# Q's and K's projections: interleaving pairs of heads in the matmul's output instead of in the cast

## The chip, the cores and the metric

The kernel runs on one core of a Trainium2 chip. The metric is the device time of one execution in microseconds, as a median over runs.

## The reference

Two branches read the same `x` (2048 rows of 512) and are mixed by a gate. Branch A is attention with a recurrent memory: 64 segments of 32 rows, 32 heads of 128, and 8 memory rows that each segment's output hands to the next.

```python
for s in range(n_seg):                       # 64 segments, one after the other
    xs = x[:, s * seg_len:(s + 1) * seg_len, :]
    h = jnp.concatenate([mem, xs], axis=1)   # 8 + 32 rows
    q = jnp.einsum('btd,dhe->bhte', h, Wq)   # 32 heads, 128 wide
    k = jnp.einsum('btd,dhe->bhte', h, Wk)
    v = jnp.einsum('btd,dhe->bhte', h, Wv)
    scores = jnp.einsum('bhqe,bhke->bhqk', q, k) * scale
    scores = jnp.where(mask, scores, -1e9)
    p = softmax(scores)
    o = jnp.einsum('bhqk,bhke->bhqe', p, v)
    o = jnp.einsum('bhte,hed->btd', o, Wo)
    mem = o[:, :M, :]                        # the next segment's memory
    outs.append(o[:, M:, :])
a = concatenate(outs)
b = gelu(layernorm(x) @ w1 + b1) @ w2 + b2
g = sigmoid((x * gate_w).sum(-1))
out = g * a + (1 - g) * b
```

## The kernel before

**Stages.** Branch B (layer norm, two matmuls, gelu) runs first, in blocks of 256 rows, while the attention weights are loaded; its result goes to `c_dr` in DRAM. Towards its end the first rows of the attention are projected between its matmuls. Then comes a loop over the 64 segments (`for s in range(nseg)`), grouped into 16 tiles `T` of four segments `si`. The order of instructions on every engine is the order of the program; no scheduler moves anything.

**Rows of a segment.** A segment has 8 + 32 = 40 rows, and a quarter of TensorE's columns takes 32. So the 8 memory rows and 24 of the segment's rows go through the loop directly (`hT`), and the other 8 rows of each of a tile's four segments, 32 in all, go together as left-over rows (`GL`). These are projected one tile ahead, as filling work between the steps of the segments: `left_qk` in the first and second segment of a tile, the output projection of the left-over rows (`wo_left`) in the third, `left_v` in the fourth.

**The projection of Q and K.** `qk_unit` (L110) computes one half (16 heads) of Q or K for 32 rows, with the rows as the stationary operand and the weights streaming through. The 128 elements of a head are cut into four parts `j` of 32, and each part has a quarter of the array's columns of its own: matmul `j` writes 512 words to partitions 32j to 32j + 31 of one PSUM bank, for 16 heads times 32 elements. Four matmuls `j` make a group, and four groups (`kc`, the four slices of 512 model columns) add up to a unit of sixteen matmuls. A segment has four units: Q and K of the first half of the heads, then Q and K of the second, in banks `U0` to `U3`. The left-over rows take four units per tile, in `X1` and `X2` (for the first tile also `U0`).

**Cast and transpose.** `qk_cast` (L115, ScalarE) casts a unit's bank to a bfloat16 tile `Tb`, in which the elements of two neighbouring heads alternate: layout (pair, element, head of the pair). In PSUM the two heads lie one after the other, 32 words each. The cast reads each partition in order and writes with a step of two elements. `qk_tr` (L119, VectorE) then transposes `Tb` as 32 x 32 blocks of four-byte words, a word being a pair of heads, into `QT` or `KT` (or `QL`; `kl_tr` at L125 into `KL` for left-over rows). Later matmuls read one head of a pair with a step of two.

**The rest of a segment, in the order of TensorE.** Mask and scores of the first half (L248, L256, L260, bank `SbF`); V's first half and a part of its second (L129); scores of the second half (bank `W`); the rest of V; the sums of the exponentials (L267, L270); P times V (L280, L285); the output projection (L141, bank `W`); the mask into `SbF`; filling work; the transposed memory rows for the next segment (L696), which take the cast `w` of the output projection (L609, ScalarE) and give `hT` (L697, VectorE), on which the next segment's L110 waits. In the first segment of a tile `out_sel` (L226), in the fourth `x_mm` (L156) stands ahead of L696. Reciprocals of the sums (L590, L655) run on VectorE; GpSimd multiplies the segment's rows by them (L601, L602), after they have been spread through DRAM (`r_dr`, `Rb`).

Of the kernel before, what the change touches and what calls it, by code (L numbers as in the profile page):

```python
# [27 lines left out]
def kernel(ctx, tc, A_x, A_mem0, A_Wq, A_Wk, A_Wv, A_Wo, A_seg_len, B_x, B_w1, B_b1, B_w2, B_b2, gate_w, out):  # L28
    nc = tc.nc
# [73 lines left out]
    W5 = (Wq5, Wk5)  # L103
# [3 lines left out]
    def qk_unit(bk, G, t, hf, kc):  # L107
        h0, h1 = HF[hf]
        for j in range(4):
            nc.tensor.matmul(bk[32 * j:32 * j + 32, :], lhsT=G[:, kc, :], rhs=W5[t][:, kc, h0:h1, j, :],  # L110
                             start=(kc == 0), stop=(kc == KC - 1), tile_position=(0, 32 * j))

    def qk_cast(bk):
        Tb = ew.tile([P, 8, 32, 2], BF16, tag="Tb", bufs=3, name="Tb")
        nc.scalar.copy(out=Tb[:].rearrange("p a e b -> p a b e"), in_=bk.rearrange("p (a b e) -> p a b e", a=8, b=2))  # L115
        return Tb

    def qk_tr(Tb, dst, hf):
# [52 lines left out]
    def left_qk(T, t, hf, bk):  # L171
        for kc in range(KC):
            qk_unit(bk, gl(T), t, hf, kc)
            if kc < KC - 1:
                yield
        def ca():
            Tb = qk_cast(bk[:])
            dve_q.append(lambda: qk_tr(Tb, QL[T % 2], hf) if t == 0 else kl_tr(Tb, T, hf))
        act_q.append(ca)
        yield  # L180
# [432 lines left out]
    for s in range(nseg):  # L613
# [17 lines left out]
        for n, (t, hf) in enumerate(((0, 0), (1, 0), (0, 1), (1, 1))):  # L631
            bk = U[n]
            for kc in range(KC):
                qk_unit(bk, hc, t, hf, kc)
            if n == 0:
                flush(act_q, 9)
                mask_mm(1)
                flush(dve_q, 9)
            qk_tr(qk_cast(bk[:]), (QT, KT)[t], hf)
# [226 lines left out]
```

## Time and profile before

| | before |
|---|---|
| median of 3 runs | 811.36 us (809.99 to 811.54) |
| the profiled execution | 808.66 us |
| its span, first to last instruction | 806.9 us |
| granted TensorE clock, mean | 0.996 |
| busy: PE / PE weight loads | 770.5 / 417.2 us |
| busy: ACT / DVE / POOL | 579.7 / 441.9 / 253.2 us |

PE is TensorE, PEld its weight loads (which overlap with its matmuls), ACT ScalarE, DVE VectorE, POOL GpSimd. Busy time counts stretches in which an engine has at least one instruction under way, so four matmuls side by side count once. The time of an execution stands beside its span: 1.8 us lie around it.

### The profile page before, as it was taken

The numbers are of one execution on the slowest core, as the hardware profiler recorded it, in microseconds if no ns is written. First come the engines' busy times: TensorE is split into PE (matmuls) and PEld (weight loads), VectorE is DVE, ScalarE is ACT, GpSimd is POOL, SyncE is SP. The second block draws the span as 40 slices with busy tenths as digits, with TensorE's granted clock in tenths as the row PEclk, the third lists the DMA queues.
The fourth block names the chain that finished last, engine by engine and source line by source line (L and its number), as shares of the span: only waits on it lengthen the run. The fifth ranks groups of instructions, "written<-read, shape, count | busy, mean of one in ns | idle before, by whom it ended". The sixth has DMA issues, their size and how long they took to land.

```text
span 806.9 us, 41225 instructions
## 1 busy us (share of the span) xinstructions
PE 770.5 (95%) x18390; PEld 417.2 (52%) x18418; DVE 441.9 (55%) x1059; ACT 579.7 (72%) x1442; POOL 253.2 (31%) x377
## 2 busy tenths in 40 slices
PE   6888999999999999999999999999999999999996
PEld 4555644555555555555555555555555555555543
DVE  5764445564646555655555565546555655555554
ACT  4554677777777777777777777877777777777773
POOL 3000013333333333333333333332333333333331
PEclk9999999999999999999999999999999999999999
DMA  6996011212122121212121222222111212121111
GB/s 190 389 381 204 28 43 48 69 63 75 69 67 77 50 66 60 85 59 85 59 84 50 61 69 76 69 70 75 57 59 59 86 60 84 60 78 59 55 57 56
DMA packets 38950, 70.41 MB, mean 87 GB/s; under 512 B 3947, under 2 KB 29136, under 8 KB 37232
## 3 DMA queue, kind: packets, MB, share of 16 engines
q1 hardware_dynamic: 38720, 67.59, 24.6%
q8 instruction: 146, 2.39, 1.2%
q14 instruction: 36, 0.29, 0.1%
q0 software_dynamic: 48, 0.13, 0.1%
HBM read 59.06 MB, written 4.45 MB: 79 GB/s over the span
## 4 chain that ended last, share of the span: by engine, by line
PE 87%; DMA 5%; ACT 4%; DVE 2%; issue 1%; SPq 0%; POOL 0%; DVEq 0%; ACTq 0%; POOLq 0%
PE U L110 28%; PE X L129 17%; PE W L141 14%; PE X L110 7%; DMA c_dr<-ct 4%; PE U L280 4%; PE X L141 3%; ACT w L609 3%; PE U L463 3%; PE W L696 2%; PE SbF L457 1%; PE W L457 1%; DMA w_sb<-in_B_w_dram 1%; PE W L256 1%; PE U L267 1%
## 5 line engine op out<-in xcount | busy, mean ns | idle before, releaser
L115 ACT CAST Tb<-U 128x512 bf16<-128x512 f32 x258 | 195.0, 757 | 42.7 <-PE U L110 24.5
L601 POOL TENSOR_TENSOR UT<-XR,Rb 128x768 bf16<-128x768 bf16 x63 | 104.8, 1664 | 239.5 <-DMA Rb<-r_dr 203.0
L110 PEld LDWEIGHTS <-hT 128*32 128x32 bf16 x4096 | 103.6, 97 | 110.3 <-DVE hT L697 19.5
L129 PE MATMUL X<-Wv_sb,hT 128*32 128x512 bf16 x2048 | 136.1, 378 | 0.0
L110 PE MATMUL U<-Wq_sb,hT 128*32 128x512 bf16 x2048 | 132.7, 379 | 1.2 <-DVE hT L697 1.2
L110 PE MATMUL U<-Wk_sb,hT 128*32 128x512 bf16 x2048 | 132.7, 379 | 0.0
L141 PE MATMUL W<-Wo_sb,UT 128*32 128x512 bf16 x2080 | 124.2, 380 | 1.5 <-ACT UT L684 1.2
L595 POOL TENSOR_TENSOR racc<-racc,R 128x320 f32<-128x320 f32 x63 | 54.5, 865 | 179.3 <-DVE R L590 175.2
L590 DVE RECIPROCAL R<-SbF 128x256 f32<-128x256 f32 x63 | 110.3, 1751 | 0.0
L119 DVE STREAM_TRANSPOSE QT<-Tb 128x256 f32<-128x256 f32 x128 | 57.0, 445 | 83.4 <-ACT Tb L115 79.7
L141 PEld LDWEIGHTS <-UT 128*32 128x32 bf16 x2080 | 56.3, 96 | 58.8 <-issue 20.6
L119 DVE STREAM_TRANSPOSE KT<-Tb 128x256 f32<-128x256 f32 x128 | 57.0, 446 | 54.0 <-ACT Tb L115 53.9
L697 DVE CAST hT<-W 128x32 bf16<-128x32 f32 x63 | 12.1, 192 | 132.6 <-PE W L696 114.4
L585 ACT CAST XR<-U 128x256 bf16<-128x256 f32 x252 | 78.6, 438 | 0.0
L609 ACT CAST w<-W 128x512 bf16<-128x512 f32 x65 | 38.0, 585 | 44.6 <-PE W L141 44.6
L684 ACT CAST UT<-U 128x64 bf16<-128x64 f32 x252 | 35.3, 227 | 43.0 <-PE U L285 43.0
L129 PEld LDWEIGHTS <-hT 128*32 128x32 bf16 x2048 | 45.6, 95 | 20.4
L115 ACT CAST Tb<-X 128x512 bf16<-128x512 f32 x62 | 46.3, 747 | 13.5 <-PE X L110 13.4
L655 DVE RECIPROCAL R<-U 128x32 f32<-128x32 f32 x126 | 44.9, 357 | 16.3 <-PE U L270 9.9
L463 PE MATMUL U<-w_sb,hTm 128*128 128x512 bf16 (+1 forms) x164 | 50.7, 387 | 1.7 <-DMA w_sb<-in_B_w_dram 1.1
L457 PEld LDWEIGHTS <-w_sb 128*128 128x128 bf16 (+1 forms) x352 | 35.0, 103 | 31.6 <-issue 13.5
L267 PEld LDWEIGHTS <-BO 128*32 128x32 bf16 x760 | 32.1, 94 | 34.8 <-issue 13.6
(148 smaller groups left out, 1191.2 us busy)
## 6 DMA issues: line engine op xcount, KB each, us to landing
Rb<-r_dr SPq DMA_DIRECT2D x63, 512.0 KB
Wq_sb<-in_A_Wq_dram SPq DMA_DIRECT2D x4, 1024.0 KB
Wk_sb<-in_A_Wk_dram SPq DMA_DIRECT2D x4, 1024.0 KB
Wv_sb<-in_A_Wv_dram SPq DMA_DIRECT2D x4, 1024.0 KB
Wo_sb<-in_A_Wo_dram SPq DMA_DIRECT2D x4, 1024.0 KB
VP<-VL SPq DMA_DIRECT2D x64, 64.0 KB
xt<-in_A_x_dram SPq DMA_DIRECT2D x16, 128.0 KB
c_dr<-ct SPq DMA_DIRECT2D x16, 128.0 KB
```

The costliest lines, as they stand in the source:

```text
L110: nc.tensor.matmul(bk[32 * j:32 * j + 32, :], lhsT=G[:, kc, :], rhs=W5[t][:, kc, h0:h1, j, :], start=(kc == 0), stop=(kc == KC - 1), tile_ ...
L115: nc.scalar.copy(out=Tb[:].rearrange("p a e b -> p a b e"), in_=bk.rearrange("p (a b e) -> p a b e", a=8, b=2))
L119: nc.vector.transpose(out=dst[:, 8 * hf:8 * hf + 8, 0:32, :].rearrange("p a r b -> p a (r b)").bitcast(FP32), in_=Tb[:].rearrange("p a e b ...
L129: nc.tensor.matmul(bk[32 * j:32 * j + 32, :], lhsT=G[:, kc, :], rhs=Wv5[:, kc, 4 * vb:4 * vb + 4, j, :], start=(kc == 0), stop=(kc == KC - ...
L141: nc.tensor.matmul(bk[32 * c:32 * c + 32, :], lhsT=U_[:, j, i, :], rhs=Wo_sb[:, 4 * i + j, :], start=(n == 0), stop=(n == NW - 1), tile_po ...
L457: nc.tensor.matmul(hp[:rows, 0:TB * P], lhsT=w1_sb[:, kc, fc * P:fc * P + rows], rhs=yTs[blk][:, kc, :], start=(kc == 0), stop=(kc == KC - 1))
L463: nc.tensor.matmul(bp(blk, tt)[:], lhsT=hTm[blk % 2][:rows, fc, tt * P:(tt + 1) * P], rhs=w2_sb[:rows, fc, :], start=(fc == 0), stop=(fc = ...
L585: nc.scalar.copy(out=XR[:, j], in_=U[j][:, 0:NG * 40].rearrange("p (i q) -> p i q", q=40)[:, :, 8:40])
L590: nc.vector.reciprocal(out=R[:, 8 * NG:], in_=SbF[:, 0:32 * NG])
L595: nc.gpsimd.tensor_tensor(out=racc[:], in0=racc[:], in1=R[:], op=ALU.add)
L601: nc.gpsimd.tensor_tensor(out=UT[(s + 1) % 2][:].rearrange("p j i q -> p (j i) q")[:, :, M:32], in0=XR[:, :, 0:RIDE], in1=Rb[:, :, 0:RIDE] ...
L609: nc.scalar.copy(out=w[:], in_=W[:])
```

## The change

The interleaving of two heads moves from the cast to the matmul. The output operand of the sixteen matmuls of a unit becomes a view of the bank as (pair, element, head of the pair), walked in the order (pair, head, element): 32 words with a step of two, then the 32 words between them. The streaming operand has the same elements in the same order, written as (pair, head, element). `qk_cast` reads the bank and writes `Tb` straight through. `Tb` holds the same values at the same places, and nothing else differs. Two added lines shift the numbers of all that follows by two, and the edited matmul is at L111 afterwards, the cast at L117.

```diff
     def qk_unit(bk, G, t, hf, kc):
         h0, h1 = HF[hf]
         for j in range(4):
-            nc.tensor.matmul(bk[32 * j:32 * j + 32, :], lhsT=G[:, kc, :], rhs=W5[t][:, kc, h0:h1, j, :],
+
+            nc.tensor.matmul(bk[32 * j:32 * j + 32, :].rearrange("p (a e b) -> p a b e", a=8, b=2), lhsT=G[:, kc, :],
+                             rhs=W5[t][:, kc, h0:h1, j, :].rearrange("p (a b) e -> p a b e", b=2),
                              start=(kc == 0), stop=(kc == KC - 1), tile_position=(0, 32 * j))
 
     def qk_cast(bk):
         Tb = ew.tile([P, 8, 32, 2], BF16, tag="Tb", bufs=3, name="Tb")
-        nc.scalar.copy(out=Tb[:].rearrange("p a e b -> p a b e"), in_=bk.rearrange("p (a b e) -> p a b e", a=8, b=2))
+        nc.scalar.copy(out=Tb[:].rearrange("p a e b -> p (a e b)"), in_=bk)
         return Tb
```

## The prediction

> **What bounds the kernel now.** I read the page's head and its slices first, then the chain that ended last, then one segment of the recurrent loop in the timeline, and last the groups and waits of the lines that the change touches. On the page the columns are busy time, share and count; the slices are fortieths of the span, in tenths.
>
> ```profile
> span 806.9 us, 41225 instructions
> PE 770.5 (95%) x18390; PEld 417.2 (52%) x18418; DVE 441.9 (55%) x1059; ACT 579.7 (72%) x1442; POOL 253.2 (31%) x377
> PE   6888999999999999999999999999999999999996
> PEclk9999999999999999999999999999999999999999
> PE 87%; DMA 5%; ACT 4%; DVE 2%; issue 1%; SPq 0%; POOL 0%; DVEq 0%; ACTq 0%; POOLq 0%
> PE U L110 28%; PE X L129 17%; PE W L141 14%; PE X L110 7%; DMA c_dr<-ct 4%; PE U L280 4%; PE X L141 3%; ACT w L609 3%; PE U L463 3%; PE W L696 2%; PE SbF L457 1%; PE W L457 1%; DMA w_sb<-in_B_w_dram 1%; PE W L256 1%; PE U L267 1%
> ```
>
> TensorE carries 87% of the chain, and the one line that the change edits on it, L110 (Q's and K's projections), carries 28 + 7 = 35% of the span. A busy PE alone does not say that it is at its pace, so I asked for the recurrent loop in one window (microseconds; busy time and count by engine) and for what PE waited for there.
>
> ```profile
> 140.00:790.00 650.00, 638.73 (x16676) 336.87 (x16694) 359.43 (x776) 491.85 (x1245) 231.51 (x316) 1.00 0.21 68
> PE W L696 <- ACT w L609: 6.5, 34, 0.6
> ```
>
> PE (first column) is busy 638.73 of 650.00 us at a granted clock of 1.00, ACT (fourth) 491.85. Of the remaining 11.3 us, 6.5 us are waits for the cast of `w`, in 34 places. Now the start of one segment, in order of time: start, length, engine, line, operation, count.
>
> ```profile
> 399.74 0.61 PE L110 MATMUL U<-Wq_sb,hT 128*32 128x512 bf16 x8
> 400.27 1.04 PE L110 MATMUL U<-Wk_sb,hT 128*32 128x512 bf16 x16
> 400.45 0.76 ACT L115 CAST Tb<-U 128x512 bf16<-128x512 f32 x1 [0.33 <-PE U L110]
> 401.13 1.04 PE L110 MATMUL U<-Wq_sb,hT 128*32 128x512 bf16 x16
> 401.41 2.44 ACT L115 CAST Tb<-U 128x512 bf16<-128x512 f32 x3 [0.20 <-PE U L110]
> 401.99 1.04 PE L110 MATMUL U<-Wk_sb,hT 128*32 128x512 bf16 x16
> 403.88 0.45 DVE L119 STREAM_TRANSPOSE KT<-Tb 128x256 f32<-128x256 f32 x1 [0.37 <-ACT Tb L115]
> 404.12 0.39 PE L129 MATMUL X<-Wv_sb,hT 128*32 128x512 bf16 x4
> 404.38 0.28 PE L256 MATMUL W<-QT,KT 128*32 128x40 bf16 x16
> 400.44 2.59 PE U L110 x48
> 411.14 2.59 PE U L110 x48
> ```
>
> A unit of sixteen L110 matmuls starts every 0.86 us (400.27, 401.13, 401.99), and the last two rows, the same piece of the chain in two successive segments, give 48 of them 2.59 us. They lie 10.7 us apart, which is the length of a segment. So a group of four, one for each quarter of the array's columns, takes 2.59 / 12 = 0.216 us, though a single one shows 0.39 us or so from start to end. The four run side by side, at 0.216 / 512 = 0.42 ns for a column. They follow one another without a gap: the projections are limited by the pace at which columns go through, not by a cast, a transpose or a load. This is the fact that decides the case. Whatever slows a column of L110 is paid in full; whatever ACT saves is paid out only where PE waits for ACT.
>
> **The change, part by part.** The program issues the same instructions in the same order on every engine; two operands change shape.
>
> *The casts.* Before, the cast reads PSUM in order and writes Tb two-byte elements four bytes apart; afterwards it is a copy in order, whose price stands in the group of another cast of this size, L609.
>
> ```profile
> L115 ACT CAST Tb<-U 128x512 bf16<-128x512 f32 x258 | 195.0, 757 | 42.7 <-PE U L110 24.5
> L115 ACT CAST Tb<-X 128x512 bf16<-128x512 f32 x62 | 46.3, 747 | 13.5 <-PE X L110 13.4
> L609 ACT CAST w<-W 128x512 bf16<-128x512 f32 x65 | 38.0, 585 | 44.6 <-PE W L141 44.6
> L256 PEld LDWEIGHTS <-KT 128*32 128x32 bf16 x2048 | 27.9, 95 | 25.2 <-DVE KT L119 16.0 <-issue 0.5
> ```
>
> (258 + 62) casts fall from some 757 to 585 ns: 320 x 0.172 = 55 us of ACT's time. What of it lies on the path? Before them ACT is idle, waiting for PE (24.5 and 13.4 us): it is the follower. The first scores of a segment need only the first two units' casts, which are done while the third and fourth run on PE. The second scores (L256 into W) need the fourth cast and its transpose, 403.88 + 0.45 = 404.33 us, and start at 404.38; the matmuls ahead of them started at 404.12 and needed 0.216 us, until 404.34. The gap is 0.04 us in each of 64 segments, 64 x 0.044 = 2.8 us, and a cast shorter by 0.17 us closes it. The weight loads' whole wait for KT, 16.0 us, is the upper bound of this gain, because most of it lies under running matmuls; the lower bound is nothing. I take 2.8 us.
>
> *The matmuls.* There are 64 segments of 4 units of 16 and, for the rows left over of each of 16 tiles, again 4 units of 16: 4096 + 1024 = 5120 L110 matmuls, 1280 groups of four. The operand that streams in has the same elements in the same order. The output goes to words 0, 2, 4, ... of a stretch of 64, then to 1, 3, 5, .... No row of the trace shows a matmul that writes so. The nearest ones:
>
> ```profile
> L110 PE MATMUL U<-Wq_sb,hT 128*32 128x512 bf16 x2048 | 132.7, 379 | 1.2 <-DVE hT L697 1.2
> L256 PE MATMUL W<-QT,KT 128*32 128x40 bf16 x1024 | 18.0, 184 | 0.0
> L280 PE MATMUL U<-E,V 32*128 32x40 bf16 x2048 | 36.3, 177 | 0.9 <-DVE E L656 0.3
> L260 PE MATMUL W<-QT,KL 128*32 128x64 bf16 x256 | 13.0, 191 | 0.0
> L270 PE MATMUL SbF<-E,BO 128*32 128x64 bf16 x256 | 13.7, 192 | 0.0
> ```
>
> From below: L256 streams its moving operand in with a step of two and takes 184 ns for 40 columns, where L280, in order, takes 177; L260 and L270 write runs of eight words with gaps between and take 191 and 192 ns for 64 columns, which is in line. Runs of eight cost nothing that can be seen, a step of two on the way in next to nothing: so the lower bound is no cost. A gain is excluded, since the number of columns stays. From above: the only write with a step of two in the trace is the old cast, and it pays for the step, 757 against 585 ns. That is 757 / 512 = 1.48 ns for a stepped element; if PSUM took stepped words no faster, a group would take 512 x 1.48 = 757 ns, 3.5 times its 216.
>
> Between these ends I take twice the time, as an estimate. A stepped pass touches its stretch of PSUM twice, with half of each pass's words left out. If a matmul's results are put away several neighbouring words at a time, be it two, four or eight, the step of two doubles the number of such writes, whatever their size, and runs of eight (the rows above) leave it as it is. If that writing is as fast as the columns come and no faster, the group takes exactly 2 x 0.216 us; if it has room to spare, less, down to nothing. The only stepped write on record pays, and PE asks for a stepped word every 0.42 ns, 3.5 times faster than that cast ever wrote one; so I lean to the full doubling.
>
> The Trainium skill speaks against this change directly: "PSUM — Partial Sum Buffer", Specifications (TRN2), gives PSUM lines of 8 bytes and says that access not in order slows matmuls considerably, and "Advanced Engine Details and Errata", PSUM Cachelines, asks for every two elements to be neighbours. By that rule the case without cost falls away and runs of eight stay free, as the L260 row has it; it names no factor, and no run here shows one for a step of two.
>
> *The sum.* 5120 / 48 x 2.59 = 276.3 us more on PE, nothing beside it to hide it: L110's idle is 1.2 us. Against it stand two small gains: 2.8 us from the scores, and part of the waits for `w`. Here the end of a tile's second segment and of its third, from the chain:
>
> ```profile
> 430.30 0.59 ACT w L609
> 430.94 0.26 PE W L696 x4
> ...
> 440.99 0.59 ACT w L609
> 441.63 0.26 PE W L696 x4
> ```
>
> L696 can't start before the cast of `w` has ended (430.30 + 0.59 = 430.89), and PE fills that time with four short mask matmuls and two groups of filling work. In the second segment of a tile these are L110 groups on the left-over rows; they get 2 x 0.216 = 0.43 us longer and cover the wait. In the third they are L141, which keeps its pace and waits on. (In the first and fourth, further matmuls stand in between.) So about half of the 6.5 us goes; with the first and last tile having no such work I take 2.9 us. DVE's transposes, POOL's products and the loads keep their length and get more room, since a segment grows from 10.7 us by 276.3 / 64 = 4.3 us.
>
> The profiled execution took 808.66 us (span 806.9); 808.66 + 276.3 - 2.8 - 2.9 = 1079.3. The median of the runs, 811.36, is 2.7 us above it; on that scale the forecast is 1082 us. About 0.2%, 1.6 us, is what a measurement of this kernel can tell from no change.
>
> **The rivals.**
>
> *The writing has room to spare: faster.* Then only the second scores' start counts, at the fourth cast of each segment: 811.4 - 2.8 = 808.6 us, at most 811.4 - 16.0 = 795.4. For it: L256's stepped operand and the runs of eight run at full pace. Against it: neither is a stepped write, and the stepped cast pays. It decides from the point where a group of four gets dearer by less than 2.8 us / 1280 = 2 ns; above that the change loses. Chance 0.16. Of it 0.05 is no change to be seen, since 2.8 us is near the 1.6 us and rests on gaps of 0.04 us read from modelled ends.
>
> *A part of the step is hidden.* If the step costs a matmul what it costs the cast, 757 / 585 = 1.29, it adds 0.294 x 276.3 = 81 us, and with the two small gains the time is 811.4 + 81 - 5.7 = 887 us. For it: it is the only price of such a step that the trace has. Against it: a cast has work of its own to hide the step beneath, while the columns come without a gap. The same would come out if only the first or only the adding matmuls of a sum were slowed. Chance 0.13, nearly all of it between 870 and 1055 us.
>
> *More than twice,* up to 811.4 + 692 (1280 x 0.541) = 1503 us, if every stepped word needs the cast's 1.48 ns: chance 0.04. ACT is a slower engine, which writes at its own pace, so its row bounds the price but is weak evidence for it.
>
> *That it doesn't do what it says* is not likely: the step is in the matmul's output operand itself, and Tb's contents are the same, so the transposes don't change.
>
> **How the numbers follow.** Doubling has 0.67: 1082 us, with its own range 1055 to 1098. Below lies a tenth of the 276.3 us that doesn't come (27 us less); above, no gain from either wait (5.7 us) and some 10 us more, since a median may lie off the profiled execution by a few times the 2.7 us seen here. With the hidden part (0.13, of which 0.12 above 870) a range of 870 to 1098 holds 0.79. It leaves out the case without cost and the one above twice. Faster by over 0.2%: 0.11, the larger part of the first rival. Within 0.2%: 0.05. Slower: 0.67 + 0.13 + 0.04 = 0.84.
>
> **What would show it.** In the new profile a unit of sixteen should start every 1.73 us instead of 0.86, a chain piece of 48 should last near 5.2 us, and the L110 group's mean should rise from 379 towards 600 ns, with L129 and L141 at 378 and 380 as before. The casts should show 585 ns and ACT's busy time should fall by some 55 us to about 525. The waits for KT before L256 should shrink, and those for `w` roughly halve. I am wrong if L110 still shows units 0.86 us apart (then the writing has room), wrong in size if they are 1.1 us apart, and wrong in the reason if L110 keeps its pace but PE sits idle before it.

## The result, and the profile after

The changed kernel takes 1069.12 us (median of 4 runs, 1068.81 to 1069.43) against 811.45 us for the kernel before: a ratio of 1.3179, 95% interval 1.3156 to 1.3202. It is slower by nearly a third, and close to the 1082 us of the forecast. The profiled execution took 1068.81 us. Its page, in the parts that were shown of before:

```profile
span 1067.0 us, 41225 instructions
PE 1035.8 (97%) x18390; PEld 466.9 (44%) x18418; DVE 440.4 (41%) x1059; ACT 531.1 (50%) x1442; POOL 252.5 (24%) x377
PEclk9999999999999999999999999999999999999999
PE 92%; DMA 4%; ACT 2%; issue 1%; DVE 1%; SPq 0%; POOL 0%; ACTq 0%; DVEq 0%; POOLq 0%
PE U L111 42%; PE X L131 13%; PE X L111 11%; PE W L143 11%; DMA c_dr<-ct 3%; PE U L282 2%; PE X L143 2%; PE U L465 2%; PE W L698 1%; PE SbF L459 1%; PE W L459 1%; ACT w L611 1%; DMA w_sb<-in_B_w_dram 1%; PE U L269 1%; PE SbF L269 1%
```

PE's busy time grew by 265 us and ACT's fell by 49; DVE, POOL and the counts stayed, and the granted clock did not fall. The edited line now carries 42 + 11 = 53% of the chain, where it carried 35%. Next the groups of the touched lines, then one segment: a timeline row of a unit, the weight loads between its groups, and a piece of the chain.

```profile
L111 PE MATMUL U<-Wq_sb,hT 128*32 128x512 bf16 x2048 | 245.9, 631 | 1.1 <-DVE hT L699 1.1
L131 PE MATMUL X<-Wv_sb,hT 128*32 128x512 bf16 x2048 | 133.1, 378 | 0.0
L143 PE MATMUL W<-Wo_sb,UT 128*32 128x512 bf16 x2080 | 125.1, 382 | 1.5 <-ACT UT L686 1.2
L117 ACT CAST Tb<-U 128x512 bf16<-128x512 f32 x258 | 151.2, 586 | 300.2 <-PE U L111 300.1
L258 PEld LDWEIGHTS <-KT 128*32 128x32 bf16 x2048 | 39.0, 105 | 38.4 <-issue 36.0
```

```profile
502.70 1.93 PE L111 MATMUL U<-Wq_sb,hT 128*32 128x512 bf16 x16
503.13 0.15 PEld L111 LDWEIGHTS <-hT 128*32 128x32 bf16 x4 [0.28 <-issue]
503.56 0.15 PEld L111 LDWEIGHTS <-hT 128*32 128x32 bf16 x4 [0.28 <-issue]
503.99 0.15 PEld L111 LDWEIGHTS <-hT 128*32 128x32 bf16 x4 [0.28 <-issue]
504.42 1.93 PE L111 MATMUL U<-Wk_sb,hT 128*32 128x512 bf16 x16
```

```profile
501.20 5.15 PE U L111 x48
```

A unit starts every 1.72 us instead of 0.86, and twelve groups take 5.15 us instead of 2.59: 0.429 us a group against 0.216, a factor of 1.99. The loads of the next group's weights, which used to follow one another closely, now come every 0.43 us and then stand idle for 0.28: all four groups of a sum are slow alike, the first, which overwrites, as well as the three that add. The matmuls of V (L131) and of the output projection (L143) keep 378 and 382 ns. A single matmul of L111 has 631 ns where it had 379; of the 252 ns more, 213 are its own stream; some 40 are left, which seem to lie at its end (the runs at odd words below show the same 0.04 us).

### The profile page after: what moved, and what is told of

The parts are those of the page before. It is cut to its first block, busy times and chain, and to the rows that moved or that the text cites. A ratio compares the mean times of both kernels' runs of the same rounds, so it can differ in the third digit from the quotient of the medians.

```text
span 1067.0 us, 41225 instructions
## 1 busy us (share of the span) xinstructions
PE 1035.8 (97%) x18390; PEld 466.9 (44%) x18418; DVE 440.4 (41%) x1059; ACT 531.1 (50%) x1442; POOL 252.5 (24%) x377
## 4 chain that ended last, share of the span: by engine, by line
PE 92%; DMA 4%; ACT 2%; issue 1%; DVE 1%; SPq 0%; POOL 0%; ACTq 0%; DVEq 0%; POOLq 0%
PE U L111 42%; PE X L131 13%; PE X L111 11%; PE W L143 11%; DMA c_dr<-ct 3%; PE U L282 2%; PE X L143 2%; PE U L465 2%; PE W L698 1%; PE SbF L459 1%; PE W L459 1%; ACT w L611 1%; DMA w_sb<-in_B_w_dram 1%; PE U L269 1%; PE SbF L269 1%
## 5 line engine op out<-in xcount | busy, mean ns | idle before, releaser
L117 ACT CAST Tb<-U 128x512 bf16<-128x512 f32 x258 | 151.2, 586 | 300.2 <-PE U L111 300.1
L111 PEld LDWEIGHTS <-hT 128*32 128x32 bf16 x4096 | 142.0, 132 | 261.7 <-issue 242.3
L111 PE MATMUL U<-Wq_sb,hT 128*32 128x512 bf16 x2048 | 245.9, 631 | 1.1 <-DVE hT L699 1.1
L111 PE MATMUL U<-Wk_sb,hT 128*32 128x512 bf16 x2048 | 244.6, 629 | 0.0
L131 PE MATMUL X<-Wv_sb,hT 128*32 128x512 bf16 x2048 | 133.1, 378 | 0.0
L143 PE MATMUL W<-Wo_sb,UT 128*32 128x512 bf16 x2080 | 125.1, 382 | 1.5 <-ACT UT L686 1.2
L143 PEld LDWEIGHTS <-UT 128*32 128x32 bf16 x2080 | 58.0, 99 | 68.8 <-issue 28.4
L111 PE MATMUL X<-Wq_sb,GL 128*32 128x512 bf16 x496 | 64.4, 615 | 0.0
L111 PE MATMUL X<-Wk_sb,GL 128*32 128x512 bf16 x496 | 64.2, 616 | 0.0
L117 ACT CAST Tb<-X 128x512 bf16<-128x512 f32 x62 | 36.5, 588 | 41.4 <-PE X L111 41.4
L258 PEld LDWEIGHTS <-KT 128*32 128x32 bf16 x2048 | 39.0, 105 | 38.4 <-issue 36.0
L131 PEld LDWEIGHTS <-hT 128*32 128x32 bf16 x2048 | 45.0, 95 | 20.7
```

Source lines behind the costliest of these rows:

```text
L111: nc.tensor.matmul(bk[32 * j:32 * j + 32, :].rearrange("p (a e b) -> p a b e", a=8, b=2), lhsT=G[:, kc, :], rhs=W5[t][:, kc, h0:h1, j, :]. ...
L117: nc.scalar.copy(out=Tb[:].rearrange("p a e b -> p (a e b)"), in_=bk)
L143: nc.tensor.matmul(bk[32 * c:32 * c + 32, :], lhsT=U_[:, j, i, :], rhs=Wo_sb[:, 4 * i + j, :], start=(n == 0), stop=(n == NW - 1), tile_po ...
L258: nc.tensor.matmul(Sb[i2][32 * j:32 * j + 32, i - 4 * i2, M:M + 40], lhsT=KT[:, h // 2, :, h % 2], rhs=QT[:, h // 2, :, h % 2], start=Fals ...
```

## The experiments

The theory: PSUM takes a matmul's results in pairs of neighbouring words, aligned to 8 bytes, one pair in the time of two columns (0.42 ns each), and a word that comes without its neighbour takes as long as a pair. The rivals are a larger unit than a pair, a price for any gap, and a price of the walk's shape rather than of the addresses. The second question is why the change cost 258 us and not the 273 us that 1280 x (0.429 - 0.216) gives.

**A larger step.** All kernels below edit the kernel before. Here Q's matmuls step by four words and K's by eight.

```diff
-            nc.tensor.matmul(bk[32 * j:32 * j + 32, :], lhsT=G[:, kc, :], rhs=W5[t][:, kc, h0:h1, j, :],
+            o = bk[32 * j:32 * j + 32, :]
+            nc.tensor.matmul(o.rearrange("p (m c) -> p c m", c=4) if t == 0 else o.rearrange("p (m c) -> p c m", c=8), lhsT=G[:, kc, :],
+                             rhs=W5[t][:, kc, h0:h1, j, :].rearrange("p (a b) e -> p b a e", b=2),
...
```

(The casts' lines, which differ for Q and K, are left out.)

> Q's matmuls write PSUM with a step of four words, K's with a step of eight, each cast reading the bank accordingly and writing Tb in order. If PSUM takes results in pairs of neighbouring words and every lone word costs one such write (0.429 us for a group of four matmuls of 512 columns, as with a step of two), both steps still give 0.43 us a group and some 1069 us in all. If it takes them four words at a time, a step of four or eight gives 0.86 us a group: some 1069 + 1280 x 0.43 = 1620 us. If eight at a time, Q's groups take 0.86 and K's 1.72 us: above 2100 us.

Measured: 1069.67 us, ratio 1.3196 (1.3156 to 1.3236). The chain piece of twelve groups, and the groups of Q (step four) and K (step eight):

```profile
412.61 5.15 PE U L111 x48
...
L111 PE MATMUL U<-Wq_sb,hT 128*32 128x512 bf16 x2048 | 245.9, 631 | 1.1 <-DVE hT L699 1.1
L111 PE MATMUL U<-Wk_sb,hT 128*32 128x512 bf16 x2048 | 244.6, 629 | 0.0
```

The rows are those of a step of two. Taken four words at a time, both groups would have been twice as slow as with a step of two; taken eight at a time, Q's twice and K's four times. So a lone word costs 0.429 us / 512 = 0.84 ns, the time of two columns, at a step of two, four or eight.

**Runs of two and of four.** The bank is walked twice, but Q leaves two words and K four together. (The matmul's output alone is shown; the streaming operand and the casts follow it.)

```diff
...
+            nc.tensor.matmul(o.rearrange("p (m b r) -> p b m r", b=2, r=2) if t == 0 else o.rearrange("p (m b r) -> p b m r", b=2, r=4), lhsT=G[:, kc, :],
+                             rhs=W5[t][:, kc, h0:h1, j, :].rearrange("p (a b) e -> p b a e", b=2),
...
```

> Q's matmuls write PSUM in runs of two words with gaps of two, K's in runs of four with gaps of four; the number of walks over the bank stays at two. Pairs of neighbouring words: both at the old pace, 0.216 us a group, 806 to 814 us in all. Four words at a time: Q's groups 0.43 us (adds about 640 x 0.213 = 136 us: some 945 us), K's 0.216. Any access with gaps is slow: both 0.43 us, some 1069 us.

Measured: 807.56 us, ratio 0.9968 (0.9949 to 0.9987).

```profile
412.52 2.59 PE U L111 x48
...
L111 PE MATMUL U<-Wq_sb,hT 128*32 128x512 bf16 x2048 | 132.8, 379 | 1.2 <-DVE hT L699 1.2
L111 PE MATMUL U<-Wk_sb,hT 128*32 128x512 bf16 x2048 | 132.7, 379 | 0.0
```

Full pace for both. Gaps of two and four words cost nothing when two or four words stay together, and neither do two walks over the bank. The 0.3% that this kernel is faster than the one before comes with its casts, which take 585 ns here instead of 757; the cast's half alone, below, gives the same 0.3% with the matmuls untouched.

**Runs of two at odd words.** Do any two neighbours do, or must they be an aligned pair? The first group of a sum goes straight through all 512 words; the other three write 448 in runs of two, Q's from word 1 on, K's from word 0.

```diff
+            o, r = bk[32 * j:32 * j + 32, :], W5[t][:, kc, h0:h1, j, :].rearrange("p (a b) e -> p b a e", b=2)
+            if kc > 0:
+                w0 = 1 if t == 0 else 0
+                o, r = o[:, w0:w0 + 448].rearrange("p (m b r) -> p b m r", b=2, r=2), r[:, :, 0:7]
...
```

> Runs of two words again, in the second to fourth group of each sum alone and for 448 of 512 columns (the first group goes straight through; the last pair of heads gets a quarter of its sum, and Q's sums are mixed up). In K's units the runs begin at even words, in Q's at odd words, so that each run straddles two aligned pairs. If PSUM takes aligned pairs (8 bytes), Q's groups of 448 columns take 0.378 us and K's 0.19: a unit of Q 1.34 us, of K 0.78 us, some 64 x 2 x (0.48 - 0.08) = 51 us and with the left-over rows 64 us more than before, near 870 us. If any two neighbours go together wherever they begin, both units take 0.78 us and the kernel 775 to 790 us.

Measured: 868.36 us, ratio 1.073 (1.0708 to 1.0751). Two units of the timeline in their order, Q and then K; the piece of the chain that holds the units K, Q, K of the same segment; and the two groups of 448 columns:

```profile
405.02 1.52 PE L114 MATMUL U<-Wq_sb,hT 128*32 128x512 bf16 x16
406.32 1.00 PE L114 MATMUL U<-Wk_sb,hT 128*32 128x512 bf16 x16
...
404.41 2.91 PE U L114 x48
...
L114 PE MATMUL U<-Wq_sb,hT 128*32 128x448 bf16 x1536 | 166.5, 567 | 0.0
L114 PE MATMUL U<-Wk_sb,hT 128*32 128x448 bf16 x1536 | 94.8, 352 | 0.0
```

K's unit takes 0.78 us (404.24 to 405.02 in the same timeline): with 0.216 for its first group, 0.19 us for each of the others. Of the chain's 2.91 us that leaves 2.91 - 2 x 0.78 = 1.35 us for Q's unit, so (1.35 - 0.216) / 3 = 0.38 us for each of its groups, as expected for two lone words in place of a pair. (The starts of the timeline, 405.02 and 406.32, lie only 1.30 us apart: the next unit's first matmul shows its start some 0.04 us before Q's last one is through, and the row behind that unit starts 0.83 us later instead of 0.78.) The same runs, one word further on, cost double: the pair is an aligned one. Q's and K's walks have the same shape here, so it is the addresses that cost, and not the shape. A long run that begins at an odd word was not measured.

The Trainium skill ("Advanced Engine Details and Errata", PSUM Cachelines) asks for every two elements to be neighbours, in lines of 8 bytes; these three runs agree with that and add the factor (0.429 us a group against 0.216). Its other sentence, that any access with gaps slows matmuls, is not borne out: runs of two aligned words ran at full pace, 0.216 us a group.

**The matmul's half of the change alone.** The casts pay for a step in Tb as before.

```diff
-        nc.scalar.copy(out=Tb[:].rearrange("p a e b -> p (a e b)"), in_=bk)
+        nc.scalar.copy(out=Tb[:].rearrange("p a e b -> p a b e"), in_=bk.rearrange("p (a e b) -> p a b e", a=8, b=2))
```

(Shown against the changed kernel.)

> The matmuls' output with a step of two as in the change, but the casts pay for a step in Tb as before (reading and writing with a step, so 757 ns or more instead of 586). If the casts are off the path, the time is that of the change, 1069 us within 2 us, ratio to before 1.317. If the 12 us by which the change came out below the pace of its matmuls were paid by the shorter casts, they are gone: some 1080 us, ratio 1.33.

Measured: 1070.38 us, ratio 1.3208 (1.3175 to 1.3241).

```profile
L116 ACT CAST Tb<-U 128x512 bf16<-128x512 f32 x258 | 190.3, 738 | 267.1 <-PE U L110 267.0
```

With 150 ns more for each cast the time is the same within the interval. The casts' gain of some 50 us of ACT's time is worth at most some 2 us here: in the chain a tile's third and fourth segments are 14.09 us long instead of 14.06, which 64 times is 1.9 us, and the wait for KT before L257 (L258 in the changed kernel) is back with 8.6 us.

**The cast's half alone.** Matmuls as before; the cast reads with a step and writes in order.

```diff
-        nc.scalar.copy(out=Tb[:].rearrange("p a e b -> p a b e"), in_=bk.rearrange("p (a b e) -> p a b e", a=8, b=2))
+        nc.scalar.copy(out=Tb[:], in_=bk.rearrange("p (a b e) -> p a e b", a=8, b=2))
```

> The matmuls as before, in order; only the cast changes: it reads PSUM with the two heads alternating (a step of 32 words) and writes Tb in order. If the cast's price was the stepped write, it falls to about 586 ns, the second scores of a segment start 0.04 us sooner, and the time falls by 2 to 4 us, to 808 us (ratio 0.995 to 0.998). If a read of PSUM out of order costs the cast as much as the stepped write did, 750 ns and more, the time stays at 811 us.

Measured: 808.12 us, ratio 0.9972 (0.9957 to 0.9988), 12 runs.

```profile
L115 ACT CAST Tb<-U 128x512 bf16<-128x512 f32 x258 | 151.1, 586 | 80.7 <-PE U L110 80.6
L256 PEld LDWEIGHTS <-KT 128*32 128x32 bf16 x2048 | 33.7, 95 | 16.6 <-issue 0.3 <-DVE KT L119 0.2
```

The cast has its 586 ns, reading words 128 bytes apart; its price had been the stepped write. The wait for KT falls from 16.0 to 0.2 us. This version has all that the change wanted for ACT, and it is the faster one: 0.28% below the kernel before, a small gain, but one whose interval leaves out 1.

**The two parts of the matmul's half, each alone.** A flag tells the left-over rows' units from the segments' own, and the step and the matching cast are used for one kind only. (Shown for the left-over rows; the other kernel has `if not left`.)

```diff
...
+            if left:
+                o, r = o.rearrange("p (a e b) -> p a b e", a=8, b=2), r.rearrange("p (a b) e -> p a b e", b=2)
...
```

> The change for the left-over rows alone (filling work of a tile's first two segments): 256 groups of four matmuls at 0.429 instead of 0.216 us, 54.6 us more matmul time. If these longer groups cover waits that stood there before (0.20 us in a tile's first segment and 0.43 in its second, as the segment lengths before and after the change suggest), 9 us of it don't come: 810.4 + 46 = 856 us, ratio 1.056. If what was gained came from elsewhere (the main units, the shorter casts), the full 54.6 us come: 865 us, ratio 1.067.

> The change for the segments' own four units alone: 1024 groups, 218.5 us more matmul time, with nothing to cover but the start of the second scores (0.044 us in 64 segments): 810.4 + 218.5 - 3 = 1026 us, ratio 1.266. If the 12 us that didn't come with the whole change were gained in these units, 1014 to 1018 us, ratio 1.252 to 1.256.

> The change itself once more, on the chip of these runs, as the base for the two kernels that make a part of it: ratio 1.317, some 1068 us. If the parts add up, the ratios of the two parts less one (0.056 and 0.266, by the first theory) add up to that of the whole less one, within 0.005.

Measured on one chip: 853.34 us and 1.0534 (1.0516 to 1.0553) for the left-over rows; 1023.71 us and 1.264 (1.2615 to 1.2666) for the segments' units; 1068.80 us and 1.3212 (1.3189 to 1.3234) for the whole. 0.0534 + 0.264 = 0.3174 against 0.3212, within 0.004: the parts add up. The left-over rows come out just below the 1.056 expected if waits are covered, the segments' units at the 1.266 expected without further gains. The table has the median length of the four segments of a tile, in us, from one mask piece of the chain (before the twelve groups) to the next:

| | first | second | third | fourth |
|---|---|---|---|---|
| before | 10.89 | 10.69 | 10.69 | 10.69 |
| cast's half alone | 10.85 | 10.65 | 10.65 | 10.65 |
| left-over rows alone | 12.43 | 11.99 | 10.69 | 10.69 |
| segments' units alone | 14.27 | 14.06 | 14.06 | 14.06 |
| the whole change | 15.81 | 15.38 | 14.06 | 14.06 |

Sixteen groups more expensive by 0.213 us are 3.41 us: the segments' units cost 3.37 to 3.38, all but the 0.04 us of the second scores. Eight are 1.71 us, but the left-over rows cost 1.54 in a tile's first segment and 1.30 in its second: 0.17 and 0.41 us are covered. Where, the chain shows; first two segments of the kernel before (a second and a third of a tile), then the same two of the kernel with the step for left-over rows alone:

```profile
427.42 0.21 PE U L280 x16
427.66 0.25 PE U L280 x16
...
438.10 0.21 PE U L280 x16
438.34 0.25 PE U L280 x16
```

```profile
407.95 0.20 PE U L286 x16
408.19 0.12 PE U L286 x16
...
419.54 0.20 PE U L286 x16
419.78 0.25 PE U L286 x16
...
PE W L702 <- ACT w L615: 4.1, 19, 0.6
```

The second half of P times V took 0.25 us where its own matmuls need 0.12: PE had been waiting there for the normalised half of E. In the kernel before, the multiplication that makes it (L656, VectorE) ends at 427.59 us and the half starts at 427.63; with the longer groups ahead of it, it has ended at 407.69 and the half starts at 408.02. That covers the 0.13 us. In the third segment, whose filling work is L141, it stays. Another 0.16 us of the second segment's 0.41 is the wait for `w`, which falls from 6.8 us in 36 places of the whole span to 4.1 us in 19. The last 0.12 us lie on either side of that wait: in the chain the output projection ahead of it takes 1.73 us instead of 1.79, and L696 (here L702) 0.19 instead of 0.26. The gains of the two segments come in some 15 tiles: 15 x (0.17 + 0.41) = 8.7 us.

## Why the prediction was right

The forecast of 1082 us lay 1.2% above the 1069.1 us measured; its range, and the narrower range of the doubling alone, hold the result. The steps, one by one:

- **What bounds the kernel.** Right. TensorE's columns set the pace, and the price of L110 was paid nearly in full: (5.15 - 2.59) / 12 x 1280 = 273 us of price, 260.1 us more span.
- **The casts.** Right in size (757 to 586 ns) and in worth: the step foresaw 2.8 us for the second scores, and the cast's half alone gained 2.3 us (0.04 us in each segment). That most of the gain for ACT would go nowhere was the main point, and the matmul's half with the old cast price shows it.
- **The doubling.** Right: 1.99. The argument that a step of two doubles the number of writes whatever their size was sound, but it left the size open; the steps of four and eight and the runs of two settle it at an aligned pair. That the writing has no room to spare, on which the full factor hangs, was a leaning (0.67) with no row of a matmul behind it; the runs bear it out. The rivals of a port with room to spare and of a partly hidden step (1.29) fall with 5.15 us for twelve groups, and so does the price of the old cast for every word: 0.84 ns, not 1.48.
- **The sum.** It came out 10.5 us too high against the profiled execution (270.6 forecast, 260.1 measured). Two terms were mis-sized. The groups' price was 273 and not 276.3 us, since a stepped group takes 0.429 us, a little less than twice 0.216: 3.3 us. The covered waits in the left-over rows' segments were 8.7 and not 2.9 us: 5.8 us. The wait for `w` itself fell by 2.7 us, as foreseen. What the term left out is the wait for E's second half, 0.13 us in two segments of 15 tiles or 3.9 us, and some 2 us on either side of the waits. The step looked for waits by name, and the wait for E hardly appears there (0.3 us in one place); the chain's 0.25 against 0.12 us tells of it. The remaining 1.4 us are the size of the differences between single segments of the kernel before, some of which were 0.1 to 0.7 us above their median, and stay open. The last 2.4 us up to 1082 are the step from the profiled execution to the median: 2.7 us were added, and 0.3 us lie between the two afterwards.
- **What would show it.** Units 1.72 us apart (1.73 foreseen), 5.15 us for 48 (5.2), a mean of 631 ns (towards 600), casts of 586 ns, the waits for KT gone and those for `w` down from 6.8 to 4.1 us. ACT's busy time fell to 531, not 525 us: the casts alone gave 241.3 - 187.7 = 53.6 us (151.2 us in U and 36.5 in X afterwards), and the other groups of ACT keep their times. Busy time counts overlapping rows once, and ACT's rows, which add up to 624 us before and 569 afterwards, overlap by 5 us less.

## What to carry to other kernels

Before moving a reordering from one engine to another, ask which of the two sets the pace: here 50 us of a follower's time were bought with 260 us of the leader's, and the same relief was to be had for nothing by reordering the cast's read of PSUM instead of its write. In the patterns run here, a matmul's output may have gaps in PSUM as long as its words go in aligned pairs; a single-word step doubles its time. And waits that the longer work would cover are found in the chain, by comparing like pieces (0.25 against 0.12 us), as well as in the list of waits.

## What the runs showed of the hardware

- Matmuls in four column strips, 512 columns: 0.216 us a group in order or in runs of two or four aligned words; 0.429 us with a step of two, four or eight words; 0.38 us for 448 columns in runs of two at odd words (0.19 at even ones). The overwriting and the adding matmuls of a sum pay alike.
- ScalarE's cast of 128 x 512 from PSUM to bfloat16: 586 ns when it writes in order, whether it reads in order or with a step of 32 words; 757 ns when it writes two-byte elements four bytes apart; 738 ns when it reads with a step of two words and writes so.
